# Attention with sinks and a window, then a gated two-layer product: the choice between two code paths is moved from the front of the kernel to its end

## The chip, the cores and the metric

The kernel runs on one core of one Trainium2 chip. The metric is the device time of one execution in microseconds (us). The core has five engines that run programs of their own and meet at semaphores: TensorE (PE; its loads of the stationary operand have a row of their own, PEld), VectorE (DVE), ScalarE (ACT), GpSimd (POOL) and SyncE (SP), which here does nothing but issue DMA transfers. A row whose engine ends in q (SPq, DVEq) shows what that engine's sequencer does by itself: issuing DMAs, loading registers, branching.

## The reference

Four sequences of 768 positions with 8 heads of 64 go through attention. A query sees the first n_sink = 4 keys and the last window = 128 keys up to itself; both numbers are inputs of the kernel. The heads side by side are the rows of x (3072 x 512), which go through a gated product of two matrices (512 x 2048 and 2048 x 512).

```python
scores = scale * np.matmul(q, k.transpose(0, 1, 3, 2))
is_sink = pos[None, :] < int(n_sink)
rel = pos[:, None] - pos[None, :]
in_window = (rel >= 0) & (rel < int(window))
scores = np.where(is_sink | in_window, scores, -1000000000.0)
scores = scores - np.max(scores, axis=-1, keepdims=True)
a = np.exp(scores)
a = a / (np.sum(a, axis=-1, keepdims=True) + 1e-09)
x = np.matmul(a, v)          # heads side by side: 3072 x 512
h = x @ w_in                 # 3072 x 2048
g = h - np.tanh(h)
out = g @ w_out              # 3072 x 512
```

## The kernel before, in words

**Two paths.** `_banded` is written for few sinks and a window of at most 128; `_general` computes the same for any numbers. The kernel loads n_sink and window into registers of all five engines (L82), works out from them whether the banded path may be taken (`bad`, L85), and branches (L94): a compare-and-branch in front of `_banded` that falls through into it, and behind `_banded` an unconditional jump past `_general` to the kernel's end (L1231). Both carry the line number L94. With this case's inputs the banded path runs.

**Units, chunks and steps.** A chunk is 256 queries of one sequence (12 chunks); a unit u is a chunk's two-head pair (4 per chunk, 48 in all). For each unit PE forms the scores (L530 for the first 12 units, which work on f32 keys and queries as they come; L537 later), VectorE merges them with the mask (L558; where a unit has keys from an earlier block, L552 first copies a triangle), ACT takes the exponential (L566), VectorE sums and inverts (L586, L587), the weights are scaled and transposed (L627), VectorE masks the transposed pieces into `pt` (L641), and PE multiplies with the values (L762, L768). ACT and VectorE split the result x into a high part xh and a low part xl (L805: two halves of a chunk, so six L805 for the first three chunks). The two-matrix part is cut in steps n = (chunk, weight group g): 24 products h (L877: xh and xl with the weights `w0_g`), tanh (L882), difference (L885), high and low part of the gate (L889, L893), then 12 products o (L929, with the weights `w1_g`); the first three steps are (chunk 0, g 0), (chunk 1, g 0), (chunk 2, g 0), step 3 is (chunk 2, g 1).

**Weights.** The matrices come packed. For each of 16 pieces (k = 0 or 1 for the matrix, g = 0 to 7) VectorE decodes in three instructions (`_decode_part`, L164, L166, L168), ACT casts the high part, VectorE subtracts it to get the low part (L854). So VectorE has four instructions of 128x1024 for each piece, all on the way to a step's products.

**What sets the order.** All this work is listed by `work.add(engine, duration, due, function, reads, writes, lands=...)`, with durations and due times in ns written by hand. `Work.order` plays it through with these numbers, each engine's time beginning at `BEGIN`, takes at each point the waiting piece with the earliest due time, and hands out one fixed order for each engine; the instructions are then issued in that order. `lands` is what a DMA issue keeps its queue busy in this model.

```python
BEGIN = {"PE": 0.0, "ACT": 500.0, "DVE": 1900.0, "POOL": 400.0, "SP": 1900.0}
...
work.add(engine, 500, t, keys, (), [slots(u)[0], "seq k"], lands=800)
work.add(engine, 1000, t, queries, (), [slots(u)[1], "seq q"], lands=600 if raw(u) else 1000)
...
work.add("DVE", 1000, 3000, rest, (), ["mask"])
```

**The start.** Ahead of `_banded`, in an order written by hand, SP loads the numbers for the masks (L74) and keys and queries of units 0 and 1 (L77 and `_load_pair`, L105: the two heads' 64 rows in two transfers), VectorE builds the parts of the masks that the first merges need, PE runs three products of the identity, and every engine loads the registers and branches. The rest of the masks (`rest`, L145 to L149, five short instructions) is a piece of `work`. On SP the values (L398), the sink values `vraw` (L452, one for each sequence, which overwrites a buffer that VectorE's L467 reads) and the packed weights follow. The 12 early units (`raw(u)`) have a DMA each for keys and two for queries (L370).

**The end.** ACT copies the last chunk's sums out of PSUM, SP stores them (L945), and each engine jumps (L94) to the closing semaphore waits of L1231.

## Time and profile before

| | |
|---|---|
| time, median of 3 runs | 650.28 us (650.25 to 650.84) |
| span of the profiled execution | 650.5 us |
| PE busy | 632.6 us (97%), 4858 products |
| DVE busy | 441.8 us (68%) |
| ACT busy | 354.7 us (55%) |
| POOL busy | 59.8 us (9%) |

The median is that of three runs; every row further down is from one profiled execution, whose span of 650.5 us is 0.2 above the median. The busy shares are averages over the span: the first 60 us, in which attention for the first three chunks and the first weights are made, and the long stretch behind them, in which PE works off steps, differ, so the rows below are cut by stretch. Instructions are pipelined, so the next one on an engine often starts a little before the one ahead of it ends; the distance from start to start is what an instruction keeps its engine.

### The profile page before, as it was taken

To read this page: it belongs to the slowest core of one execution; us is meant where nothing else is said; L and a number is where in the kernel's file an instruction comes from. 1 tells how busy PE (TensorE), PEld (TensorE's weight loads), DVE (VectorE), ACT (ScalarE), POOL (GpSimd) and SP (SyncE) were. 2 spreads that over 40 slices of the span, in tenths; PEclk is the share of its full clock that TensorE was granted. 3 is DMA by queue.
4 is the path that set the end of the run, shared out by engine and by line. 5 is a ranking of instruction groups with operands and counts; after the bars stand their busy time and mean duration, and the time that the engine had idled before them with its cause. 6 is when DMAs were issued, how large, how long until landed. Compare 5 with 4: busy or idle time off the path is not lost.

```text
span 650.5 us, 13450 instructions
## 1 busy us (share of the span) xinstructions
PE 632.6 (97%) x4858; PEld 563.9 (87%) x4858; DVE 441.8 (68%) x1169; ACT 354.7 (55%) x949; POOL 59.8 (9%) x191
## 2 busy tenths in 40 slices
PE   7799999999999999999999999999999999999996
PEld 4467999998989999999989989989999999889995
DVE  6999999957976676856767766666676675642221
ACT  4774444447856556646557557566565565532221
POOL 3663100000000010000010000001000000000000
PEclk9899999999999999999999999999999999999999
DMA  6789920013544344234234233334242342210001
GB/s 199 255 271 333 369 80 0 2 62 108 157 123 151 82 123 146 76 97 143 76 110 151 72 101 117 92 101 120 86 130 86 102 123 66 82 50 1 33 1 37
DMA packets 75350, 73.45 MB, mean 113 GB/s; under 512 B 21132, under 2 KB 62732, under 8 KB 75276
## 3 DMA queue, kind: packets, MB, share of 16 engines
q1 hardware_dynamic: 74972, 72.18, 35.9%
q8 instruction: 40, 0.66, 0.4%
q10 hardware_dynamic: 304, 0.33, 0.2%
q14 instruction: 34, 0.28, 0.1%
HBM read 55.58 MB, written 16.91 MB: 111 GB/s over the span
## 4 chain that ended last, share of the span: by engine, by line
PE 85%; DVE 4%; SPq 3%; ACT 3%; DMA 2%; issue 1%; POOL 1%; ACTq 0%; DVEq 0%; POOLq 0%
PE o L929 38%; PE h L877 36%; PE s L537 5%; PE x L789 4%; DMA turned<-pt 1%; PE x L768 1%; ACT p L566 1%; ACT p L597 1%; DMA qk<-qd 1%; SPq L684 1%; PE s L530 1%; PE x L779 1%; DVE p L558 1%; DMA z<-sinks 1%; PE t L627 1%
## 5 line engine op out<-in xcount | busy, mean ns | idle before, releaser
L877 PE MATMUL h<-xh,w 128*128 128x256 f32 x1536 | 275.6, 277 | 0.0
L877 PEld LDWEIGHTS h<-xh,w 128*128 128x128 f32 x1536 | 237.4, 188 | 2.8 <-issue 1.0
L877 PE MATMUL h<-xl,w 128*128 128x256 f32 x768 | 212.2, 276 | 0.0
L929 PE MATMUL o<-w,gh 128*128 128x512 f32 x768 | 194.0, 393 | 1.1 <-DVE w L854 0.5
L929 PEld LDWEIGHTS o<-w,gh 128*128 128x128 f32 x768 | 137.3, 188 | 27.2 <-issue 1.4
L877 PEld LDWEIGHTS h<-xl,w 128*128 128x128 f32 x768 | 144.3, 188 | 1.7
L885 DVE TENSOR_TENSOR h<-h,graw 128x512 f32<-128x512 f32 x96 | 66.5, 692 | 67.4 <-ACT graw L882 67.3
L566 ACT ACTIVATE p<-p,st 128x132 f32<-128x132 f32 x192 | 76.3, 398 | 53.0 <-DVE st L558 51.4
L929 PE MATMUL o<-w,gl 128*128 128x512 f32 x384 | 103.0, 390 | 0.0
L882 ACT ACTIVATE graw<-h 128x512 f32<-128x512 f32 x96 | 57.2, 596 | 76.4 <-PE h L877 75.9
L893 DVE TENSOR_TENSOR gl<-h,gh 128x512 fp32r<-128x512 f32 x96 | 65.5, 683 | 34.0 <-ACT gh L889 33.9
L889 ACT CAST gh<-h 128x512 fp32r<-128x512 f32 x96 | 55.9, 582 | 57.9 <-DVE h L885 57.9
L929 PEld LDWEIGHTS o<-w,gl 128*128 128x128 f32 x384 | 71.9, 188 | 15.2
L552 DVE COPY_PREDICATED s<-above,s 128x256 f32<-128x256 uint32 x76 | 32.4, 426 | 48.5 <-PE s L537 46.4
L558 DVE CUSTOM_DVE_ANT_0 p<-s,mask 128x132 f32<-128x132 f32 x192 | 48.9, 292 | 8.2 <-PE s L530 2.8
L602 POOL CAST z<-p 128x16 fp32r<-128x16 f32 x48 | 11.3, 236 | 455.1 <-ACT p L597 386.6
L597 ACT ACTIVATE p<-p,st 128x132 f32<-128x132 f32 x144 | 46.6, 394 | 7.6 <-DVE st L587 6.9
L537 PEld LDWEIGHTS s<-ks,q 128*128 128x128 f32 x288 | 42.3, 188 | 5.3 <-issue 0.8
L537 PE MATMUL s<-ks,q 128*128 128x260 f32 x288 | 46.0, 283 | 0.7 <-DVE ks L494 0.5
L494 DVE TENSOR_TENSOR ks<-kraw,ks 64x392 fp32r<-64x392 f32 x72 | 40.5, 562 | 2.3
L499 ACT CAST q<-qraw 128x512 fp32r<-128x512 f32 x36 | 22.4, 623 | 32.6 <-PE s L537 29.2
L489 ACT CAST ks<-kraw 64x392 fp32r<-64x392 f32 x72 | 37.2, 517 | 0.9
(87 smaller groups left out, 503.9 us busy)
## 6 DMA issues: line engine op xcount, KB each, us to landing
qraw<-qd SPq DMA_DIRECT2D x36, 256.0 KB, 2.7
turned<-pt SPq DMA_DIRECT2D x36, 256.0 KB, 2.0
pt<-turned SPq DMA_DIRECT2D x144, 64.0 KB, 2.0
wraw<-w_in SPq DMA_DIRECT2D x16, 512.0 KB, 7.5
wraw<-w_out SPq DMA_DIRECT2D x16, 512.0 KB, 6.1
kraw<-kp SPq DMA_DIRECT2D x37, 196.0 KB, 2.7
out<-ob SPq DMA_DIRECT2D x24, 256.0 KB, 2.5
v<-vp SPq DMA_DIRECT2D x42, 128.0 KB, 2.9
```

Of the source, the lines that this page charges most:

```text
L489: nc.scalar.copy(ks[u][r, h, :], kt[u][r, :])
L494: nc.vector.tensor_tensor(k[o, h, :], t[r, :], k[r, h, :].bitcast(F32), op=ALU.subtract)
L537: nc.tensor.matmul(ps[h][:, :WIN], lhsT=q[:, h, t * P : (t + 1) * P], rhs=rhs, start=i == 0, stop=i == 1,)
L558: nc.vector.tensor_tensor_reduce(out=pr[u][:, j, :], in0=ps[h][:, P:WIN], in1=mask[:, kind, :], scale=-0.125, scalar=BIG, op0=ALU.add, op1 ...
L566: nc.scalar.activation(e, e, AF.Exp, bias=st[u][:, j : j + 1], scale=-1.0, accum_out=st[u][:, 4 + j : 5 + j],)
L597: nc.scalar.activation(pr[u][:, j, :], pr[u][:, j, :], AF.Copy, scale=s[:, 8 + j : 9 + j])
L877: nc.tensor.matmul(y, lhsT=w, rhs=x, start=r == 0, stop=r == 11)
L882: nc.scalar.activation(gr[n], hps[n], AF.Tanh)
L885: nc.vector.tensor_tensor(hps[n], hps[n], gr[n], op=ALU.subtract)
L889: nc.scalar.copy(gh[n], hps[n])
L893: nc.vector.tensor_tensor(gl[n], hps[n], gh[n].bitcast(F32), op=ALU.subtract)
L929: nc.tensor.matmul(y, lhsT=(gh, gh, gl)[i][n][:, f, t * P : (t + 1) * P], rhs=w, start=first and not low and r == 0, stop=bool(last and lo ...
```

## The change

The register loads and the choice of path move behind `_banded`, which now always runs; `_general` runs behind it if the numbers ask for it, and overwrites the output. The queries of the 12 early units come in one transfer of 128 rows. In the planner SP and VectorE begin at 0, and an early unit's query load counts 500 instead of two times 600.

```diff
@@ tile_attention_moe_kernel
-            _load_pair(nc, q, qd[0, 2 * m : 2 * m + 2, :, :CH])
+            _load_pair(nc.sync, q, qd[0, 2 * m : 2 * m + 2, :, :CH])
...
-        _, (nlo, nhi, wlo, whi) = nc.values_load_multi_w_load_instructions(
-            nsw[0:1, 0:4], skip_runtime_bounds_check_because="every value takes one of the two branches"
-        )
-        bad = nhi | whi | ((nlo + 3) >> 3) | ((wlo - 1) >> 7)
...
-    with tc.If(bad == 0) as cmp:
-        _banded(tc, qd, kp, vp, vs, masks, w_in, w_out, ident, pts, early, out)
-    with cmp.Else():
+    _banded(tc, qd, kp, vp, vs, masks, w_in, w_out, ident, pts, early, out)
+    with tc.manual_schedule(engines={et.PE, et.SP, et.DVE, et.Activation, et.Pool}):
+        _, (nlo, nhi, wlo, whi) = nc.values_load_multi_w_load_instructions(
+            nsw[0:1, 0:4], skip_runtime_bounds_check_because="every value takes one of the two branches"
+        )
+        bad = nhi | whi | ((nlo + 3) >> 3) | ((wlo - 1) >> 7)
+    with tc.If(bad != 0):
         _general(tc, qd, kp, vp, nswi, w_in, w_out, ident, xd, out)
@@ _load_pair
-def _load_pair(nc, q, src):
-    for h in range(2):
-        r = slice(64 * h, 64 * h + 64)
-        nc.sync.dma_start(q[r], src[h, r])
+def _load_pair(engine, q, src):
+    engine.dma_start(q, src.rearrange("h r s -> (h r) s")[P // 2 : P // 2 + P])
@@ Work
-    BEGIN = {"PE": 0.0, "ACT": 500.0, "DVE": 1900.0, "POOL": 400.0, "SP": 1900.0}
+    BEGIN = {"PE": 0.0, "ACT": 500.0, "DVE": 0.0, "POOL": 400.0, "SP": 0.0}
@@ load_qk
                 if raw(u):
-                    for h, r in enumerate(HALF):
-                        queue.dma_start(qt[u][r], src[h, r])
+                    _load_pair(queue, qt[u], src)
...
-            work.add(engine, 1000, t, queries, (), [slots(u)[1], "seq q"], lands=600 if raw(u) else 1000)
+            work.add(engine, 500 if raw(u) else 1000, t, queries, (), [slots(u)[1], "seq q"], lands=500 if raw(u) else 1000)
```

The new numbers make the planner hand out another order for the first steps. In the rows that follow, of the programs as they are issued, the changed kernel's line numbers are lower by 2 (mask and decode code: L162, L164, L166 stand for L164, L166, L168) or by 3 (L638 for L641, L765 for L768, L802 for L805, L851 for L854, L874 for L877, L890 for L893, L926 for L929). In names, `w0_1` is the first matrix's group 1, `xl2` is xl of chunk 2, `x2_2` its second half in PSUM, `h2` and `h3` belong to steps 2 and 3, and numbers behind the last underscore only count buffers.

VectorE around the last of the six L805, before:

```order
L166 SCALAR_TENSOR_TENSOR pt_60<-wraw0_1_494,pt_60 128x1024
L893 TENSOR_TENSOR gl1_943<-h1_793,gh1_923 128x512
L168 SCALAR_TENSOR_TENSOR pt_60<-wraw0_1_494,pt_60 128x1024
L164 TENSOR_SCALAR pt_60<-wraw1_1_609 128x1024
L805 TENSOR_TENSOR xl2_884<-x2_2_909,xh2_883 128x512
L166 SCALAR_TENSOR_TENSOR pt_60<-wraw1_1_609,pt_60 128x1024
L854 TENSOR_TENSOR w0_1_957<-pt_60,w0_1_957 128x1024
L168 SCALAR_TENSOR_TENSOR pt_60<-wraw1_1_609,pt_60 128x1024
L164 TENSOR_SCALAR pt_60<-wraw0_2_708 128x1024
```

The same place on VectorE after the change (`w0_1`'s L851 stands some way ahead of the first row here):

```order
L802 TENSOR_TENSOR xl2_794<-x2_0_723,xh2_793 128x512
L890 TENSOR_TENSOR gl1_830<-h1_612,gh1_804 128x512
L164 SCALAR_TENSOR_TENSOR pt_60<-wraw1_1_412,pt_60 128x1024
L638 TENSOR_TENSOR pt_60<-t11_834,below_77 128x2x128
L638 TENSOR_TENSOR pt_60<-t11_834,after_78 128x2x128
L166 SCALAR_TENSOR_TENSOR pt_60<-wraw1_1_412,pt_60 128x1024
L162 TENSOR_SCALAR pt_60<-wraw0_2_511 128x1024
L164 SCALAR_TENSOR_TENSOR pt_60<-wraw0_2_511,pt_60 128x1024
L851 TENSOR_TENSOR w1_1_874<-pt_60,w1_1_874 128x1024
L802 TENSOR_TENSOR xl2_794<-x2_2_839,xh2_793 128x512
```

Both matrices' group 1 and the first two decode instructions of group 2 now stand ahead of the second half of `xl2`; before, only a part of group 1 did.

PE at the second half of chunk 2's values product, before:

```order
L762 MATMUL x2_2_909<-zr_260,vsink_257 128x512
L768 MATMUL x2_2_909<-pt_60,v2_0_800 64x256 x2
L768 MATMUL x2_2_909<-pt_60,v2_1_802 64x128 x2
L768 MATMUL x2_2_909<-pt_60,v2_0_800 64x256 x2
L768 MATMUL x2_2_909<-pt_60,v2_1_802 64x128 x2
L929 MATMUL o1_948<-w1_0_860,gh1_923 128x512
L929 MATMUL o1_948<-w1_0_860,gh1_923 128x2x8x32
L929 MATMUL o1_948<-w1_0_860,gh1_923 128x512 x6
L929 MATMUL o1_948<-w1_0_860,gl1_943 128x512 x4
L877 MATMUL h2_925<-xh2_883,w0_0_537 128x256
L877 MATMUL h2_925<-xl2_884,w0_0_537 128x256
L877 MATMUL h2_925<-xh2_883,w0_0_537 128x256 x2
```

The same place on PE after the change:

```order
L759 MATMUL x2_2_839<-zr_174,vsink_171 128x512
L765 MATMUL x2_2_839<-pt_60,v2_0_672 64x256 x2
L765 MATMUL x2_2_839<-pt_60,v2_1_674 64x128 x2
L765 MATMUL x2_2_839<-pt_60,v2_0_672 64x256 x2
L765 MATMUL x2_2_839<-pt_60,v2_1_674 64x128 x2
L926 MATMUL o1_825<-w1_0_532,gl1_830 128x512 x2
L874 MATMUL h3_881<-xh2_793,w0_1_753 128x2x4x32
L874 MATMUL h3_881<-xl2_794,w0_1_753 128x256
L874 MATMUL h3_881<-xh2_793,w0_1_753 128x256 x2
L874 MATMUL h3_881<-xl2_794,w0_1_753 128x256
L874 MATMUL h3_881<-xh2_793,w0_1_753 128x256
L874 MATMUL h2_842<-xh2_793,w0_0_359 128x256
```

Ten of the twelve `o1` products now stand ahead of `x2_2`, and six of step 3's products, which use the first half of `xl2`, stand between it and the remaining products of step 2, which use the second half.

SP at the end, before:

```order
L945 DMA out<-ob11_0_7872 128x512
L945 DMA out<-ob11_1_7877 128x512
L94 UNCONDITIONAL_BRANCH
L1051 DMA graw0_0_7907<-w_in 128x2048
L1051 DMA graw1_0_7913<-w_out 128x2048
```

And after (what follows here, as above, is the general path):

```order
L942 DMA out<-ob11_0_7776 128x512
L942 DMA out<-ob11_1_7781 128x512
L92 TENSOR_LOAD nsw_ptr
L92 TENSOR_LOAD nsw
L96 REGISTER_ALU
L96 ISA
L96 REGISTER_ALU
L96 ISA
L96 REGISTER_ALU
L96 COMPARE_AND_BRANCH
```

The two register loads and the branch that stood ahead of the first values on SP now stand behind the last store, and the compare-and-branch is the one that leads past the general path.

## Rows read from the trace of the kernel before

**Rows 1.** First line of the page.

```profile
span 650.5 us, 13450 instructions
```

**Rows 2.** Busy time by stretch: us and instructions of each engine, clock, DMA share, GB/s.

```profile
0.00:8.60 8.60, 4.80 (x18) 3.57 (x18) 4.78 (x31) 2.17 (x5) 2.06 (x12) 1.00 0.47 122
8.60:62.32 53.72, 47.37 (x323) 32.66 (x320) 48.57 (x182) 37.74 (x135) 29.09 (x59) 0.97 0.87 288
62.32:160.00 97.68, 97.68 (x650) 89.40 (x649) 84.41 (x122) 45.57 (x84) 2.29 (x6) 1.00 0.31 105
160.00:644.67 484.67, 482.76 (x3875) 438.22 (x3873) 304.02 (x838) 268.66 (x726) 26.36 (x114) 1.00 0.32 95
```

**Rows 3.** Timeline of PE: start, duration, line, operation, out<-in, count.

```profile
4.97 2.44 PE L530 MATMUL s<-pt 64*128 64x260 f32 x8
...
63.65 0.28 PE L877 MATMUL h<-xh,w 128*128 128x256 f32 x1
...
68.60 0.63 PE L929 MATMUL o<-w,gh 128*128 128x512 f32 x2
```

**Rows 4.** Chain of waits in order of time, its start: start, duration, what.

```profile
2.29 0.59 SPq L105
...
4.71 1.19 SPq L82
...
7.04 0.34 SPq L398
```

**Rows 5.** Timeline of VectorE at its first merge, idle time before it in brackets.

```profile
7.23 0.30 DVE L558 CUSTOM_DVE_ANT_0 p<-s,mask 128x132 f32<-128x132 f32 x1 [2.32 <-PE s L530]
...
7.67 0.22 DVE L145 COPY mask<-mask 128x128 f32<-128x128 f32 x1
```

**Rows 6.** VectorE's waits from 0 to 62.32: us in total, times, longest.

```profile
DVE p L558 <- PE s L530: 2.8, 2, 2.3
DVE s L552 <- PE s L530: 1.7, 3, 1.1
...
DVE pt L641 <- ACT pt L634: 1.0, 2, 0.5
```

**Rows 7.** Timeline of VectorE around the sixth L805.

```profile
61.03 0.69 DVE L164 TENSOR_SCALAR pt<-wraw 128x1024 uint32<-128x1024 uint32 x1
61.63 0.68 DVE L805 TENSOR_TENSOR xl<-x,xh 128x512 fp32r<-128x512 f32 x1
62.23 1.22 DVE L166 SCALAR_TENSOR_TENSOR pt<-wraw,pt 128x1024 uint32<-128x1024 uint32 x1
63.36 1.22 DVE L854 TENSOR_TENSOR w<-pt,w 128x1024 fp32r<-128x1024 f32 x1
64.50 1.22 DVE L168 SCALAR_TENSOR_TENSOR pt<-wraw,pt 128x1024 uint32<-128x1024 uint32 x1
```

**Rows 8.** Timeline of SP at the end.

```profile
643.95 1.69 SPq L945 DMA_DIRECT2D out<-ob  x2
```

**Rows 9.** Single lines: duration in ns (least/median/most), first and last start.

```profile
L945 SPq DMA_DIRECT2D out<-ob x24: 332/356/377, 142.8 to 645.3; - x24
...
DMA to landing us min/median/max: 2.0/2.5/4.3
...
L82 ACTq TENSOR_LOAD <-nsw x1: 1578/1578/1578, 1.6 to 1.6; - x1
...
L82 SPq TENSOR_LOAD <-nsw x1: 507/507/507, 5.9 to 5.9; - x1
...
L94 SPq COMPARE_BRANCH  x2: 38/46/53, 6.9 to 645.7; - x2
L94 DVEq COMPARE_BRANCH  x2: 50/56/63, 7.0 to 641.3; - x2
...
L1231 SPq EVENT_SEMAPHORE  x8: 17/28/28, 648.6 to 650.4; - x8
...
L1231 DVEq DRAIN  x2: 10/25/40, 644.2 to 650.0; - x2
```

## The prediction

> **What bounds the kernel now.** I read the page's first line first: the profiled execution spans 650.5 us [rows 1], 0.2 above the median of 650.28; all sums below are made against 650.5 and brought down by 0.2 at the end. Then busy time by stretch [rows 2]: the reader is to see that PE is busy for all 97.68 us from 62.32 to 160, and idle for only 1.91 of the 484.67 us after that. From 62 us on PE is the bound and simply works off its list. Whatever the change is worth in front is therefore read at one question: at what time does PE stand where it stood at about 64 us? Before that, VectorE is the fuller engine: it has idled 3.82 us by 8.60, and from there to 62.32 it is busy 48.57 of 53.72 us, 90%, while its last piece of attention for this stage still lies ahead of PE's [rows 2].
>
> The last thing PE needs from attention in this stage is the second half of xl of chunk 2 (the sixth L805). In the kernel before PE did not wait for it: it went on at 63.65 behind other work, with 18 products of step 2 and 24 of step 3 to do until 68.60, 0.118 us each [rows 3].
>
> **The change part by part.**
>
> The register loads and the branch in front go. On SP's part of the chain the loads start at 4.71 and the next transfer starts at 7.04: 2.33 us in which SP issues nothing [rows 4]. On VectorE a wait of 2.32 us stands before the first merge at 7.23, and the profile puts it down to PE [rows 5]. But VectorE's own branch is at 7.0 [rows 9], while PE began the first four products at 4.97 and took 2.44 us [rows 3], so the first two were there at about 6.2. The gap is VectorE's loads, and the merge can start about 0.95 us earlier. Besides, the rest of the masks (five short instructions from 7.67 to 8.60, where the first stretch of [rows 2] ends, 0.93 us [rows 5]) now stands ahead of that merge, where VectorE has nothing to do anyhow. Together VectorE gains 1.9 us at the start. The loads on PE, ACT and POOL cost nothing before: PE waits there for unit 0's data, ACT for scores, POOL has no work; their removal gives nothing.
>
> A pair's early queries in one transfer instead of two: one issue of about 0.6 us less per unit on SP (the second half's issue at 2.29 took 0.59 [rows 4]). For units 0 and 1 it brings data some tenths earlier, but PE's products at low speed follow each other without a gap there; I count nothing beyond the 0.95 above. Later units' transfers are issued well ahead, so these savings lie under VectorE's work.
>
> The planner. Because a query load is now half as long for it, and SP and VectorE begin at 0 in its model, it hands out another order up to step 6. That is the largest term, and it is read from the order of VectorE. Ahead of the sixth L805 stand the same instructions as before and six more, all of them weight work: one L164, two L166, one L168, two L854. From the kernel before: an L164 keeps VectorE for 0.60 us (61.03 to 61.63), an L166 for 1.13 (62.23 to 63.36), an L854 for 1.14 (63.36 to 64.50), and an L168 is taken like the L854 [rows 7]. That is 0.60 + 2 x 1.13 + 3 x 1.14 = 6.3 us. The sixth L805 ended at 61.63 + 0.68 = 62.3; with these ahead it ends at 68.6, less what VectorE idles less.
>
> What it idles less has two parts. The 1.9 us of the start are as good as certain. Of the later waits for another engine, the longest of the three kinds are 1.1, 0.5 (2.8 less the 2.3 of the start) and 0.5 us [rows 6], 2.1 in all; the order around them is another one, the weight work that comes earlier can stand where VectorE waited, but new waits of that kind can come. The first units stay a chain from product to merge to exponential and keep their short ones. I count half, 1.05. The bounds: none of it, so 1.9; all waits of the three kinds, 0.5 + 1.7 + 1.0 = 3.2 more, so 5.1. With 2.95 the sixth L805 ends at 65.65, and PE goes on 0.1 later, at 65.75.
>
> In the new order PE has by then done six products of step 3 that came later before, so the same amount of work was left to it at 63.65 + 6 x 0.118 = 64.36. PE's whole remaining list is therefore 1.4 us later (bounds 2.4 later and 0.7 earlier). Before the step moved, PE's cover for xl was the second half of step 1; that cover now runs out some 2 us before xl is there. Behind it PE's order is the old one, and VectorE, with its weights done earlier, is no longer close behind PE, so I let the shift stand until the end. The 1.91 us of PE idle after 160 I leave as they are.
>
> The end. Every engine now loads the registers and branches after its last instruction. For PE, ACT, VectorE and POOL this starts earlier than SP's and is covered by it. SP ends its last store's issue at 643.95 + 1.69 = 645.64 [rows 8]. Before, its jump is at 645.7 and its next instruction at 648.6, 2.9 us on; the last store, issued at 645.3, lands up to 4.3 us later, at 649.6, and ends the kernel 0.9 us after that [rows 9]. So the jump lay under the landing. Now SP runs the loads first, 2.33 us as at the start [rows 4], and then jumps: 645.64 + 2.33 + 2.9 = 650.9. That is 1.3 us after the landing, and the short semaphore waits that were passed under it, 0.2 to 0.3 us, come on top: 1.6 us. VectorE jumps alike, from 641.3 to 644.2 with nothing to wait for [rows 9], so the 2.9 us are the jump and not a wait. Bounds: above, one load took 1.58 us on ACT and 0.51 on SP [rows 9], 1.1 more, so 2.7; below, the branch in front that is not taken (6.9 on SP, next transfer at 7.04 [rows 4, 9]) costs 0.1, SP would be through at 648.1 under the landing, and the end would cost nothing. I take 1.6, since the jump at the end leads past the same general path as the one measured there.
>
> [...]
>
> One wait changes its place. On SP the third load of vraw, which waits for VectorE's L467, stands ahead of unit 8's keys and queries now (before: behind unit 9's). Behind it in SP's queue are units 8 and 9 and the weights of group 2. VectorE has between that L467 and unit 8's first merge an L805, an L168, an L854 and the merges and masks of unit 7, which cover most of a transfer's issue and landing. I count nothing and keep it for the upper side; uncovered, I put it at 1 to 2 us, a choice.
>
> Sum: 650.5 + 1.4 + 1.6 = 653.5 for a profiled execution, less 0.2: **653.3 us**, slower by 0.46%.
>
> **The rivals.** (0.2%, 1.3 us, is about what a measurement of this kernel can tell from no change.)
>
> *The start's chain carries through* (faster). SP's part of the chain gets shorter by 2.33 us of loads and by four issues of second halves of 0.6 us (units 0, 1, 3 and 4) [rows 4], 4.7 us. If the transfers, and not VectorE, set the pace until 62 us, all of that reaches PE, and with the end's 1.6 us the time is 647.2. For it speaks that the chain runs over SP up to unit 5's load; against it that VectorE is busy 90% of the time from 8.60 on and has 6.3 us more to do first. It decides where the sixth L805 ends before about 61.4.
>
> *The end is hidden, or VectorE makes up nearly everything.* If the jump is short, 651.7; if VectorE saves 4.5 to 5.1 us, 651.1 to 651.7; both together would be no change. The 1.91 us of PE's late waits may also shrink and lead here.
>
> *VectorE saves nothing beyond the start, or waits anew* for unit 8's loads: PE is 2.4 us later or, with 1 to 2 us for the loads, 3.4 to 4.4; the time is 654.3 to 656.3.
>
> *The new order does nothing* to PE's pace, because weight work fills waits that were there anyway: only the end counts, 651.9. It needs 4.3 us of waits saved, more than the start gives.
>
> **How the numbers follow.** Forecast as worked out (652 to 655): 0.56. End hidden, VectorE making up nearly everything, or the order without effect (650.3 to 652): 0.23, of which 0.15 within 0.2%. More waits (above 654.3, half of it above 655.4): 0.13. Chain carried through: 0.08. So faster 0.08, within 0.2% 0.16, slower 0.76. The range 650.6 to 655.4 leaves out the faster case, a few hundredths of the second and half of the third, under 0.2.
>
> **What would show it.** The first merge at about 6.3 us with the masks' rest ahead of it; the sixth L805 ending between 65 and 67 us, with a PE wait of 1 to 2 us before the next L877; step 2's first L929 at about 70 instead of 68.6; PE without waits from there to 160; the last L929 ending about 1.4 us later; on SP some 2.3 us of loads after the last store's issue, then 2.9 us to its next record, which now comes after the landing. The prediction is wrong if the sixth L805 ends before 64 us or after 68, or if SP's record after the branch is there before the last store lands.

## The result, and the profile after

The changed kernel takes 659.31 us (median; 658.87 to 659.79) against 650.28: slower by 9.0 us, ratio 1.0133 (95% interval 1.0119 to 1.0148; the two medians by themselves give 1.0139). The forecast was 653.3, and the range ended at 655.4.

The profiled span grows from 650.5 [rows 1] to 656.9, so the two traces hold 6.4 us of the 9.0. The rest lies in the baseline: in the runs beside the experiments each execution of the kernel before took 1.77 to 1.96 us more than its own span, 1.85 on average (a span of 650.5 went with 652.35 us), so the profiled execution, whose own time is not on record, was by this one of the longer ones, 2.1 above the median; the changed kernel's takes 2.2 more than its span (659.14 at 656.9), 0.4 more than before's. 6.4 + 2.1 + 0.4 + 0.2 (659.31 over 659.14) are the 9.0, but for roundings.

First line of the changed kernel's page, to set beside [rows 1]:

```profile
span 656.9 us, 13426 instructions
```

Busy time by the stretches of [rows 2], same columns:

```profile
0.00:8.60 8.60, 3.96 (x16) 2.94 (x18) 5.06 (x31) 1.85 (x4) 1.86 (x12) 1.00 0.64 206
8.60:62.32 53.72, 42.10 (x288) 29.80 (x287) 48.55 (x179) 36.84 (x133) 29.34 (x57) 0.94 0.80 277
62.32:160.00 97.68, 96.85 (x644) 87.43 (x643) 79.76 (x106) 42.16 (x70) 5.33 (x6) 1.00 0.28 97
160.00:644.67 484.67, 483.45 (x3895) 439.84 (x3894) 307.29 (x853) 272.64 (x740) 27.40 (x117) 1.00 0.32 96
```

The loss is made before 62 us: PE does 42.10 us of work there instead of 47.37, VectorE is as busy as before (48.55 against 48.57). Behind 62 us PE works off its list as before.

Timeline of PE: the first scores, the wait for xl, and step 2's first L926 (L929 in [rows 3]); the idle time before an instruction stands in brackets:

```profile
6.29 2.10 PE L527 MATMUL s<-pt 64*128 64x260 f32 x8 [2.38 <-DMA pt<-qd]
...
69.73 0.39 PE L874 MATMUL h<-xl,w 128*128 128x256 f32 x1 [0.67 <-DVE xl L802]
...
74.14 1.20 PE L926 MATMUL o<-w,gh 128*128 128x512 f32 x4 [0.16 <-ACT gh L886]
```

Timeline of VectorE at the first merge [rows 5] and at the sixth xl [rows 7]:

```profile
5.55 0.22 DVE L143 COPY mask<-mask 128x128 f32<-128x128 f32 x1
...
7.69 0.29 DVE L555 CUSTOM_DVE_ANT_0 p<-s,mask 128x132 f32<-128x132 f32 x1 [0.93 <-PE s L527]
...
67.86 1.22 DVE L851 TENSOR_TENSOR w<-pt,w 128x1024 fp32r<-128x1024 f32 x1
68.99 0.68 DVE L802 TENSOR_TENSOR xl<-x,xh 128x512 fp32r<-128x512 f32 x1
```

The masks' rest (L143) did move ahead, but the first scores begin at 6.29 instead of 4.97, held by the landing of unit 0's queries, and the first merge at 7.69 instead of 7.23. The sixth xl ends at 68.99 + 0.68 = 69.67 instead of 62.31; PE waits 0.67 us for it, reaches step 2's L926 5.5 us later than before (74.14 against 68.60), and its last product ends 4.8 us later (649.45 against 644.66).

VectorE's busy time from 0 to the end of the sixth xl, the kernel before first, the changed kernel second (columns as in [rows 2]):

```profile
0.00:62.31 62.31, 52.16 (x337) 36.23 (x338) 53.34 (x211) 39.90 (x140) 31.16 (x71) 0.97 0.81 265
```

```profile
0.00:69.67 69.67, 52.81 (x349) 37.97 (x349) 59.90 (x217) 41.94 (x143) 34.55 (x73) 0.95 0.73 248
```

So up to this point VectorE worked 59.90 - 53.34 = 6.56 us more in six more instructions, and idled 69.67 - 59.90 = 9.77 us where it had idled 62.31 - 53.34 = 8.97.

The end, by single lines (duration in ns, first and last start), to set beside [rows 9]:

```profile
L942 SPq DMA_DIRECT2D out<-ob x24: 332/357/1304, 148.4 to 650.1; - x24
...
L92 SPq TENSOR_LOAD <-nsw_ptr x1: 1067/1067/1067, 650.5 to 650.5; - x1
L92 SPq TENSOR_LOAD <-nsw x1: 602/602/602, 651.6 to 651.6; - x1
...
L96 SPq EVENT_SEMAPHORE  x8: 17/17/17, 655.2 to 655.7; - x8
...
L96 SPq COMPARE_BRANCH  x1: 54/54/54, 652.6 to 652.6; - x1
...
L1228 SPq EVENT_SEMAPHORE  x8: 17/28/28, 655.8 to 656.9; - x8
```

The store is issued at 650.1, two loads take 1.67 us, the branch is at 652.6 and SP's next record at 655.2, eight semaphore steps follow, and the kernel ends at 656.9: 7.5 us behind PE's last product, where it was 5.8.

### The profile page after: what moved, and what is told of

Read it like the earlier page. It is cut to its first block, busy times and chain, and to the rows that moved or that the text cites. A ratio compares the mean times of both kernels' runs of the same rounds, so it can differ in the third digit from the quotient of the medians.

```text
span 656.9 us, 13426 instructions
## 1 busy us (share of the span) xinstructions
PE 631.1 (96%) x4858; PEld 563.6 (86%) x4858; DVE 442.0 (67%) x1169; ACT 355.3 (54%) x949; POOL 63.9 (10%) x191
## 4 chain that ended last, share of the span: by engine, by line
PE 85%; DVE 6%; ACT 4%; issue 1%; SPq 1%; DMA 1%; POOL 1%; ACTq 0%; DVEq 0%
PE o L926 38%; PE h L874 36%; PE s L534 5%; PE x L786 4%; ACT p L563 1%; PE s L527 1%; DVE p L555 1%; ACT p L594 1%; DVE pt L164 1%; DMA pt<-qd 1%; PE x L776 1%; DVE pt L166 1%; DVE s L549 1%; DVE pt L638 1%; PE x L765 0%
## 5 line engine op out<-in xcount | busy, mean ns | idle before, releaser
L874 PE MATMUL h<-xh,w 128*128 128x256 f32 x1536 | 277.1, 278 | 0.0
L874 PEld LDWEIGHTS h<-xh,w 128*128 128x128 f32 x1536 | 238.5, 189 | 2.1 <-issue 0.3
L874 PE MATMUL h<-xl,w 128*128 128x256 f32 x768 | 212.7, 277 | 0.7 <-DVE xl L802 0.7
L926 PE MATMUL o<-w,gh 128*128 128x512 f32 x768 | 193.4, 393 | 0.3 <-ACT gh L886 0.2
L926 PEld LDWEIGHTS o<-w,gh 128*128 128x128 f32 x768 | 137.4, 188 | 25.9 <-issue 1.0
L874 PEld LDWEIGHTS h<-xl,w 128*128 128x128 f32 x768 | 144.8, 189 | 2.5 <-DVE xl L802 0.9
L926 PE MATMUL o<-w,gl 128*128 128x512 f32 x384 | 103.2, 390 | 0.0
L890 DVE TENSOR_TENSOR gl<-h,gh 128x512 fp32r<-128x512 f32 x96 | 65.6, 683 | 34.7 <-ACT gh L886 34.6
L926 PEld LDWEIGHTS o<-w,gl 128*128 128x128 f32 x384 | 71.9, 188 | 15.3 <-issue 0.2
```

Source lines behind the costliest of these rows:

```text
L874: nc.tensor.matmul(y, lhsT=w, rhs=x, start=r == 0, stop=r == 11)
L890: nc.vector.tensor_tensor(gl[n], hps[n], gh[n].bitcast(F32), op=ALU.subtract)
L926: nc.tensor.matmul(y, lhsT=(gh, gh, gl)[i][n][:, f, t * P : (t + 1) * P], rhs=w, start=first and not low and r == 0, stop=bool(last and lo ...
```

## The experiments

The first theories: A, the new order puts weight work ahead of the sixth xl, and so PE is late; B, the loss comes from the start, where transfers collide; C, the time outside the span grows with the branch at the end. Later came F (weight work ahead of the fifth xl), H (SP's order) and L (the lead of the scores over the rest of the attention). "Order" below is what the planner hands out. Each time stands beside runs of the kernel before on the same chip; ratios are to those.

**The branch alone at the end.** The kernel before with these two pieces behind `_banded`:

```diff
-        _, (nlo, nhi, wlo, whi) = nc.values_load_multi_w_load_instructions(...)
-    with tc.If(bad == 0) as cmp:
+    _banded(...)
+    _, (nlo, nhi, wlo, whi) = nc.values_load_multi_w_load_instructions(...)
+    with tc.If(bad != 0):
```

> The kernel before, with nothing but the register loads and the branch moved behind the banded path; query loads, planner numbers and so every engine's order are those of before. Theory A (the new order of VectorE's weight work made the loss, PE 4.8 us later at its last instruction): PE ends within 1 us of before (644.7), the span grows by the tail alone, 1.65 us, to 651 to 652.5. Theory B (without the loads in front the first transfers run into each other, and the start is what was lost): PE ends at about 649, the span is about 656. For the 2.2 us by which the changed kernel's time exceeds its span: theory C (they come with the branch at the end) has time minus span at about 2.2 here; theory D (they come from the order or the transfers) has it at -0.2.

653.47 us, ratio 1.0040 (1.0025 to 1.0054); PE's last product ends at 644.1, the tail is 7.7, time minus span 2.1. The move by itself costs 2.7 us, and PE, without the loads in front, is hardly earlier (644.1 against 644.66).

**The branch alone back in front.** The changed kernel with loads and branch in the old place.

> The changed kernel with the register loads and the branch put back in front; the new planner numbers, its order and the merged query transfers stay. Theory A: PE's last instruction ends 4 to 7 us later than before, the span is 655 to 657 with before's tail. Theory B: the start is before's, PE ends within 1 us of before, span 650 to 651.5. Theory C: time minus span -0.2. Theory D: 2.2.

658.44 us, 1.0104 (1.0077 to 1.0131); PE's last product ends at 651.9, the sixth xl at 72.5. Most of the loss stays, and the sixth xl is no earlier than in the changed kernel: the loss is made by the new order and not, as theory B had it, at the start.

**The old numbers.** The changed kernel with BEGIN and query loads as the planner had them before, so with the old order.

> The changed kernel with the planner numbers of before (1900 at the start, 1000 and 600 for a query load), so with before's order on every engine; branch at the end and merged query transfers stay. Theory A: like the kernel with only the branch moved, span 651 to 652.5. Theory B: span about 656, and, if the merged transfers are what collides, longer than with two transfers. Theory C: time minus span 2.2. Theory D: -0.2 if the order is at work, 2.2 if the transfers are.

653.69 us, 1.0043 (1.0026 to 1.0059), like the branch alone. One transfer for a pair's queries is worth nothing that can be measured here, and the new order costs some 5.6 us, 659.3 less 653.7.

**No branch.** Loads, branch and general path left out; the kernel computes the banded path alone.

> The changed kernel without register loads, branch and general path (it computes the banded path alone). Both theories on PE: PE ends as in the changed kernel, at about 649.5; the tail is before's or shorter, so the span is 655 to 655.3, 1.65 to 2 less than the changed kernel's 656.9. Theory C: time minus span goes back to -0.2, so the time is about 655. Theory D: it stays at 2.2, the time is about 657.4.

654.27 us, 1.0052 (1.0036 to 1.0067). PE is as late as expected (last product 650.6), but the tail is 3.7 us, shorter than before's 5.8: without the jump past the general path the kernel ends about 2 us sooner behind PE than the kernel before, which has it (1.4 to 2.7, since the tail is 5.0 to 6.3 us in the three traces with the branch in front). Time minus span went to 1.8, so theory C; but it is a small term, 2.1 to 2.2 with the branch at the end and 1.85 in the kernel before.

**The register loads earlier**, with the old order, the branch still at the end:

```diff
+LATE = 40
...
+            for i, n in enumerate(todo):
+                if i == len(todo) - LATE:
+                    bad = _choice(nc, nsw)
                 work.all[n][3]()
```

> The kernel with the order and transfers of before and the branch behind the banded path, its register loads moved ahead of the last 40 pieces of the planner's list, so on SP ahead of the last two stores, where SP waits for ACT anyway; branch and jump stay at the end. If the tail is the chain of SP's loads (1.67 us), their arithmetic (0.4) and the jump (2.6), the tail gets 2.1 us shorter than with the loads behind the store (7.7), so 5.6, and the time is 651.1 to 651.7. If the store's landing or the jump alone ended it, the tail stays above 7 and the time at 653 to 653.7. Should PE, VectorE or ACT be held up by their own loads, PE's end moves up to 2 us later and the time is 652 to 653.5 with a tail of 5.6.

652.06 us, 1.0027 (1.0013 to 1.0042); the tail is 5.8, where 5.6 was forecast for loads and jump in a row, and the time is a little above the forecast.

**ScalarE holds back unit 2's loads**, on top of the last one:

```diff
+                if u == 2:
+                    nc.scalar.copy(gap[:, 0:1], qt[0][:, 0:1])
                 queue.dma_start(kt[u], ...)
```

> The kernel with the old order, branch at the end and early register loads (652.06), with one thing more: ScalarE copies one column of unit 0's queries before it issues unit 2's loads, so these start after unit 0's data have landed, as they started later in the kernel before (3.85 us). If these loads in the way of unit 0's were what ate the gain at the start, unit 0's first product starts at 4.9 to 5.3 instead of 6.0, the first merge at 6.4 to 6.9 instead of 7.7, the sixth xl ends about 1 us earlier than 62.0 and the time is 650.8 to 651.4. If SP's own next transfers (values, weights) are what is in the way, the first product stays at 5.9 or later and the time at 652.

651.44 us, 1.0008 (0.9991 to 1.0025). Timeline of PE:

```profile
4.54 2.96 PE L537 MATMUL s<-pt 64*128 64x260 f32 x8 [0.63 <-DMA pt<-qd]
```

Unit 0's data come 1.5 us earlier (4.54 against 6.0) and the first merge starts at 6.8 instead of 7.7: unit 2's loads, which ScalarE issues from 0.75 us on when it has no registers to load, were in the way. But the sixth xl ends at 62.6 (62.0 without). A first merge that is 0.9 us earlier did not reach it. This is the best version with the branch at the end, and no faster than the kernel before.

**The second weight groups behind the sixth xl**, for the planner alone, in the changed kernel (the planner makes its whole list anew, and the calls that list the attention of chunks 1 and 2 move ahead of these weights):

```diff
+                first = [("xu", 2, 2)] if (k, g) in ((1, 1), (0, 2)) else []
-                ... bits(i), [("wr", k, g, 0), ("wr", k, g, 1)], ...
+                ... bits(i), [("wr", k, g, 0), ("wr", k, g, 1)] + first, ...
```

> The changed kernel with one dependence added for the planner alone: the decoding of weight groups (second matrix, 1) and (first matrix, 2) may only start behind the second half of xl of chunk 2. Ahead of the sixth xl subtraction VectorE then has 12.0 us of weight instructions instead of 17.7 (11.4 in the kernel before), the order up to group 1's first piece stays the changed kernel's. Theory A (the weight work ahead of this xl is what delays PE, about 1 us per us): the sixth xl ends near 64, PE ends 5 to 6 us earlier, time 653 to 654.5. Theory E (the rest of the new order, its waits at the first units, lost the time): less than 1.5 us is won, time 657.8 to 659.5.

660.31 us, 1.0139 (1.0103 to 1.0174). VectorE up to the end of the sixth xl:

```profile
0.00:69.37 69.37, 54.72 (x346) 39.01 (x347) 54.09 (x211) 40.52 (x142) 31.61 (x72) 0.93 0.73 247
```

Theory A, on which the forecast stood, falls: 5.8 us of work were taken away (54.09 against 59.90), and the xl is there at 69.37 instead of 69.67. The work's place was filled with idle time (15.3 us).

**Only a part of the new numbers.** The zero start with the old query loads:

> The changed kernel with the old planner numbers for a query load (1000 and 600) and the new zero start of SP and VectorE. Its order has 14.8 us of weight instructions ahead of the sixth xl subtraction, 2.9 less than the changed kernel's and 3.4 more than before's. Theory A: time between the changed kernel's 659.3 and the 653.6 of the kernel with the old order, at 656 to 657.5. Theory E: no order in it; as likely near 659 as near 653.6.

658.62 us, 1.0129 (1.0101 to 1.0158): above theory A's interval. VectorE's zero start alone:

> The changed kernel with only VectorE's start in the planner at 0; SP's start and the query loads have the numbers of before. 10.8 us of weight instructions stand ahead of the sixth xl subtraction, 0.6 less than before. Theory A: 652.5 to 654, like the kernel with the old order or half a us better. Theory E: any other time, since the order of the first units is another one again.

654.63 us, 1.0071 (1.0048 to 1.0095). Less weight work ahead goes with less time among these plans, but not throughout: this one has 0.6 us less of it than the old order (1.0043) and is no faster, and the run before these two has 5.7 us less than the changed kernel and takes as long. No cause is shown by this.

**The kernel before again.**

> The kernel before, unchanged, for a second profile of it. The forecast was made against a profiled execution with a span of 650.5 us; the other executions of the same kernel had spans of 648.0 to 651.0 and times 1.85 us above their spans. If the first profile was one of the long ones, this one has a span near 648.7, its granted clock is nearer to 1, and PE ends about 1 us earlier than 644.7, the tail is under 5.8. If it was typical, all of these are as in the first profile.

651.03 us beside 651.08, ratio 1.0002. The second profile has again a span of 650.5, at a clock of 0.991; its time is 652.35 and the eight executions have spans of 648.2 to 651.6. The first profile was thus a usual one of the longer half, and it is the time outside the span that the forecast had overlooked.

**The first weight group behind the fifth xl as well.**

> As the kernel whose second weight groups wait for the sixth xl (660.3 us), and the decoding of group (first matrix, 1) waits for the fifth xl as well: 8.0 us of weight instructions ahead of the fifth xl instead of 12.0 (before: 8.6), the same 12.0 ahead of the sixth. Theory F (weight instructions that stand between the merges and sums of the units ahead of the fifth xl lengthen attention's chain; those between the fifth and the sixth lie in a wait): the fifth xl ends 3 to 4 us earlier than the 62.8 there, the sixth 2.5 to 4 earlier than 69.4, the time is 656 to 657.8. Rival E (the first units' order and the start): less than 1 us is won.

661.93 us, 1.0161 (1.0139 to 1.0183). The fifth xl came 3.4 us earlier (59.4), as theory F said, the sixth 1.7 later (71.1): in this run's plan six products of step 3 stand ahead of chunk 2's second values product (in the changed kernel they stand behind it), and PE waited 0.75 us in them for these weights. Theory F's time is missed.

**PE filled in its two long waits**, in the changed kernel:

```diff
+                for _ in range(8 if u in (5, 9) else 0):
+                    nc.tensor.transpose(ps[:, 0, 0, :], ident, ident)
```

> The changed kernel with eight transposes of the identity put ahead of the transposes of units 5 and 9, where PE waits 2.4 and 2.6 us for GpSimd; their results are overwritten by those that follow. Theory G (PE's low clock after these two waits, 0.5 from 34.0 to 37.4 and from 51.1 to 54.5, slows the products on the chain to the sixth xl): the low stretches go, the sixth xl ends 1.5 to 3 us earlier, time 656.5 to 658. Theory F (the waits are a result of VectorE's order and the low clock costs little): time within 1 us of 659.3.

657.70 us, 1.0101 (1.0082 to 1.0120), some 2 us less than the changed kernel (1.0133 on both chips it ran on). In the changed kernel the granted clock is 0.50 in these two stretches, at PE's waits of 2.41 us (to 32.93) and 2.60 us (to 51.72) for GpSimd (columns as in [rows 2], the clock is the third number from the end):

```profile
34.01:37.40 3.39, 3.14 (x14) 2.75 (x16) 2.65 (x6) 1.51 (x4) 2.57 (x4) 0.50 0.58 137
51.07:54.47 3.40, 2.75 (x13) 2.75 (x14) 3.18 (x11) 1.73 (x9) 1.25 (x4) 0.50 0.99 336
```

The first wait was not filled: the fill products themselves had to wait, 2.41 us for VectorE until 33.18, and the low stretch is there as it was (32.75 to 36.14). At the second place the wait is 1.38 us ahead of them, and the low stretch is gone. The sixth xl ends at 69.0, where two profiles of the changed kernel have 69.67 and 70.47.

What the clock is worth can also be read from executions with different clocks. Of the ten without a branch the two with a mean clock of 0.999 and more took 652.5 and 652.7 us, the eight at 0.992 653.9 to 656.2. But the second profile of the kernel before has 10.2 us at 0.50 ahead of its sixth xl, which ends at 62.94 even so; and one profile of a kernel further down (weights as before, SP's new order) has none, and its xl ends at 68.06. In that order:

```profile
0.00:62.94 62.94, 52.27 (x337) 36.27 (x338) 53.49 (x211) 39.86 (x140) 31.06 (x71) 0.92 0.82 269
```

```profile
0.00:68.06 68.06, 51.54 (x343) 34.91 (x343) 52.95 (x211) 40.89 (x142) 32.09 (x72) 1.00 0.75 252
```

The clock is a part of the loss, not the main part.

**SP's part of the order against the other engines'.** A list made of two plans, SP's rows from the plan with the old numbers, or all but SP's:

```diff
+    rows = {e: [n for n in (old if e in OLD else new) if work.all[n][0] == e] for e in w.BEGIN}
```

> The changed kernel, its order on PE, VectorE, ScalarE and GpSimd, but on SP the order of transfers that the numbers of before give: the third sink-value load behind units 8 and 9 instead of ahead of them, weights spread between the units' loads. Theory H (SP's order made the loss: units 8 to 11 were issued at 34.1, 36.0, 38.4 and 47.7 us in the changed kernel, at 28.2, 28.9, 33.1 and 34.5 by the old order, and the last halves of attention wait for them): the sixth xl ends 3 us or more earlier than 69.7, time 655 to 656.5. Theory F (the compute engines' order, VectorE's weight work ahead of the fifth xl): less than 1 us is won, 658.3 to 659.5. Both chains equally long: 657 to 658.3, since each holds when the other is mended.

> The other way round: the order of before on PE, VectorE, ScalarE and GpSimd, the changed kernel's order of transfers on SP alone; branch at the end, merged query loads. Theory H: most of the loss is here, 657 to 659.5. Theory F: like the kernel with the old order everywhere (653.7), 653.3 to 654.5. Both chains: 655 to 658.

> The changed kernel once more, on the chip of these two, as the corner with which they are compared, and for a second profile: 658.5 to 659.8, sixth xl at 69 to 70.5, unit 11's keys issued at 47 to 49 us.

On one chip: 658.71 (1.0112, 1.0079 to 1.0146) with SP's old order, 667.14 (1.0256, 1.0225 to 1.0287) with SP's new order alone, 660.14 (1.0133, 1.0108 to 1.0159) with both. So the compute engines' order costs about 5 us by itself (653.7 to 658.7), SP's in the changed kernel some 1.4 more, which the intervals do not tell from nothing. With the old compute order SP's new one costs 13. PE there:

```profile
39.62 2.10 PE L552 MATMUL s<-qk 64*128 64x260 f32 x8 [4.71 <-DMA qk<-qd]
...
57.54 2.02 PE L552 MATMUL s<-qk 64*128 64x260 f32 x8 [4.41 <-DMA qk<-qd]
```

PE waits 4.71 and 4.41 us for the keys and queries of units 8 and 11. The changed kernel's SP, whose order this is, issues unit 8's at 34.07, behind the third sink-value load, and unit 11's at 47.66; the kernel before issues them at 23.66 and 36.72. Changed kernel first, then before:

```profile
33.46 0.56 SPq L449 DMA_DIRECT2D vraw<-vs  x1
34.07 0.46 SPq L356 DMA_DIRECT2D qk<-kp  x1
...
47.66 0.42 SPq L356 DMA_DIRECT2D qk<-kp  x1
```

```profile
23.66 0.43 SPq L358 DMA_DIRECT2D qk<-kp  x1
...
36.72 0.43 SPq L358 DMA_DIRECT2D qk<-kp  x1
```

**Weights as before, attention in a new order** (the one that the planner makes with these ties and the new numbers; it is neither the old one nor quite the changed kernel's), with the order on SP that the old numbers give and with the one that the new ones give:

```diff
+BEHIND = {(0, 0): (0, 0, 1, 1), (1, 0): (2, 3, 4, 4), (0, 1): (4, 5, 5, 6), (1, 1): (5, 6, 6, 6), (0, 2): (6, 6, 6, 6)}
```

> The changed kernel with SP's order of the numbers of before, and VectorE's weight instructions bound, for the planner, to the same places between the six xl subtractions as in the kernel before: 2, 4, 5, 6, 9 and 12 of them ahead of the first to the sixth xl (changed kernel: 3, 6, 8, 10, 13, 18). What stays new is the order of the attention pieces themselves, as the planner makes it with a zero start. Theory F (the weight instructions among the units' merges and sums make the five us that the compute engines' order costs): the sixth xl ends at 62 to 64.5, time 653.5 to 655.5. Rival K (the order of the attention pieces is what costs): the sixth xl stays at 67 or later, time 657 or more.

> The same with the changed kernel's own order on SP. Theory H2 (behind VectorE's work the late loads of units 8 to 11 are a second chain of nearly the same length, hidden in the changed kernel and open once VectorE is quick): time at least 3 us above the run with SP's old order, 657 to 663, with PE waiting 2 to 5 us for a unit's queries. If SP's order does no harm by itself: within 1 us of that run.

662.33 us, 1.0166 (1.0133 to 1.0198), and 662.39, 1.0177 (1.0149 to 1.0205): neither is nearer to the kernel before than the changed kernel is. VectorE up to the end of the sixth xl with the old numbers on SP:

```profile
0.00:71.28 71.28, 57.87 (x343) 38.34 (x343) 53.32 (x211) 40.80 (x142) 32.55 (x72) 0.95 0.70 240
```

It does the work of before (53.32 us in 211 instructions, before 53.34 in 211) and idles 71.28 - 53.32 = 17.96 us. Its waits in that time (us in total, times, longest):

```profile
DVE xl L829 <- ACT xh L825: 3.7, 1, 3.7
DVE pt L665 <- PE t L651: 2.0, 1, 2.0
DVE pt L665 <- ACT pt L658: 1.6, 3, 0.7
DVE p L582 <- POOL z L626: 1.6, 1, 1.6
```

The sixth xl itself now waits 3.7 us for ScalarE. So the weight work that stands ahead is not the sole cause (theory F falls), and with the weights in their old place SP's order makes no difference in time.

**The lead of the scores**, with SP's old order:

```diff
+        for u in range(RAW - 2):
+            work.all[made["t", u]][4].update(made["s", u + 2, t] for t in range(2))
```

> The kernel with the new compute order and SP's old order (658.7), with one thing more bound for the planner: PE may transpose a unit's weights only behind the scores of the unit two further on, as it did in the kernel before nearly throughout (s4 before t2, s8 before t6, s11 before t9; in the new order s4 behind t2, s8 behind t6, s11 behind t9). The planner then puts 19.4 us of weight instructions ahead of the sixth xl subtraction, more than the changed kernel's 17.7. Theory L (what the new order took is the lead of the scores: unit 11's scores began at 55.9 us instead of 46): unit 11's scores begin 3 us or more earlier than 56.9, the sixth xl ends 3 us or more earlier than 70.7, time 653.5 to 656. Theory F (weight instructions ahead of the xl subtractions): the sixth xl at 70 or later, time 658.5 or more.

The last scores of the stage (unit 11's) on PE, in the kernel before, the changed kernel and this one:

```profile
45.80 1.15 PE L530 MATMUL s<-qk 64*128 64x260 f32 x8
```

```profile
55.91 1.15 PE L527 MATMUL s<-qk 64*128 64x260 f32 x8
```

```profile
55.33 0.71 PE L552 MATMUL s<-qk 64*128 64x260 f32 x4 [0.23 <-DVE st L580]
```

In the changed kernel PE makes them 10.1 us later than before. Tied two units ahead, as here, they are hardly earlier (this is their second half), and PE waits for VectorE in front of them. 662.46 us, 1.0182 (1.0152 to 1.0212). VectorE up to the sixth xl, first without the tie (the run with SP's old order), then with it:

```profile
0.00:70.66 70.66, 53.84 (x349) 38.41 (x349) 59.77 (x217) 41.81 (x143) 34.49 (x73) 0.95 0.72 244
```

```profile
0.00:71.64 71.64, 56.27 (x347) 38.82 (x348) 61.72 (x218) 41.63 (x144) 31.25 (x73) 0.95 0.71 239
```

Its idle time fell from 70.66 - 59.77 = 10.89 to 71.64 - 61.72 = 9.92 us, but more work came ahead of the xl, 61.72 - 53.34 = 8.38 us over before. Theory L's forecast is missed; since the last scores did not really come earlier, this does not clear them either.

## Why the prediction was wrong

Its frame held. In every run PE's last product ends 579 to 583 us behind the sixth xl, a spread of 4 us over all orders (before 644.66 - 62.31 = 582.35, changed 649.45 - 69.67 = 579.78), so what counts is when that xl is there. What failed is the step that put it there at 65.65.

**The step that failed.** The forecast added 6.3 us of weight work and took off 2.95 us of saved idle time. The work was sized right: 6.56 us. Of the idle time nothing was saved; it rose by 0.80. The xl came 7.36 us later instead of 3.3, and PE's list was 5.5 us late at step 2's L926 and 4.8 at the last product instead of 1.4. That is 3.4 of the 6.0 us by which the forecast missed.

Nor was VectorE's list ahead of the xl, from which this sum was made, the path that set its time. In every trace the sixth xl starts 0.7 to 1.7 us behind the end of PE's second values product of chunk 2 (L768, now L765), with only ScalarE's xh between them. Before and after the change:

```profile
59.34 1.52 PE L768 MATMUL x<-pt,v 128*64 128x256 f32 x16
60.90 0.59 ACT L801 CAST xh<-x 128x512 fp32r<-128x512 f32 x1 [1.94 <-PE x L768]
```

```profile
66.08 1.52 PE L765 MATMUL x<-pt,v 128*64 128x256 f32 x16
67.65 0.59 ACT L798 CAST xh<-x 128x512 fp32r<-128x512 f32 x1 [0.55 <-PE x L765]
```

The product ends at 67.60 instead of 60.86: 6.74 of the 7.36 us, and VectorE's list adds 0.62. So PE is late before the xl is. Up to the sixth xl PE works 0.65 us more (52.81 against 52.16 in the lines of the section on the result) and idles 16.86 us instead of 10.15. GpSimd scales a unit's weights before PE transposes them, and PE's waits for it there, of which the kernel before lists none, are 7.4 us:

```profile
PE t L624 <- POOL p L589: 5.0, 3, 2.6
PE t L624 <- POOL z L599: 2.4, 1, 2.4
```

The second values product of chunk 0 still ends earlier than before (28.16, before 30.02), the next one later (40.16, 38.07), with the wait of 2.41 us between them; from the second of chunk 1 (47.46, 45.87) to the first of chunk 2 (58.94, 53.46), around the wait of 2.60 us, 3.9 us more are lost. GpSimd itself waits 25.6 us for VectorE's inverses, where it waited 14.9. That weight work delays PE by this way round is read from the trace and not shown by a run: with the scores tied two units ahead PE's waits for GpSimd are down to 0.2 us, others have come, and the xl is as late.

- The 1.9 us of the start, "as good as certain", did not come. The masks' rest did move, but without ScalarE's loads its queue issues unit 2's transfers at 0.75 us, into unit 0's landing. Holding them back showed that (first product at 4.54 instead of 6.0); it also showed that an earlier first merge did not bring the sixth xl earlier, and that VectorE's loads were only a part of the gap: with none in front, and PE's first product 0.43 us earlier than before, the first merge came at 6.78, 0.45 us earlier than before and not 0.95.
- "Half of the later waits" had the wrong sign. In VectorE's waits up to the sixth xl of the changed kernel (columns as in [rows 6]) those for PE are shorter (2.6 us instead of 4.5, with the start's 2.3 gone), those for ScalarE longer (2.6 instead of 1.6), and waits on a DMA and on POOL are new. A line of the kernel before that [rows 6] do not show stands first:

```profile
DVE st L586 <- ACT p L566: 0.6, 2, 0.3
```

```profile
DVE p L555 <- PE s L527: 2.4, 4, 0.9
DVE pt L638 <- ACT pt L631: 1.7, 3, 1.0
...
DVE st L583 <- ACT p L563: 0.9, 2, 0.7
DVE few L134 <- DMA nswi<-nsw: 0.9, 1, 0.9
DVE vsink L464 <- POOL vraw L460: 0.5, 1, 0.5
DVE s L549 <- PE s L527: 0.2, 1, 0.2
```

- Deeper, work and idle time are not two terms. Taking 5.8 us of the work away gave 5.5 us more idle time (54.09 busy, 15.28 idle), taking all of it away 8.2 more than in the changed kernel (53.32 and 17.96), and with the scores tied 1.0 us less idle time came with 1.95 us more work. In all three the sixth xl starts 0.7 to 0.8 us behind PE's values product (68.68, 70.59 and 70.96, behind 68.01, 69.92 and 70.18): what VectorE has no longer to do ahead of the xl, it waits. Of the orders tried, only the old one (the sixth xl at 62.0 to 62.9 in its runs) and the one with VectorE's zero start alone (63.6) have it near its old time.

**What stands, what is open.** The new order of the compute engines costs some 5 us by itself, SP's in the changed kernel perhaps 1.4 more. The branch behind the banded path costs 2.7 us with the order as before. The merged transfer is worth nothing measurable by itself. Which move within the compute engines' order is decisive is open: the weights alone were put back and gave nothing, the attempt on the scores did not make them early, both together were put back only as the whole old order, and no run took away PE's waits for GpSimd by themselves. The low clock at PE's two waits is a part of it; one run with fill products puts half of it at some 2 us, with intervals that touch.

**The end.** The forecast was 1.6 us; the tail grew by 7.49 - 5.81 = 1.68. That this is so near is in part luck. The tail of one and the same program differs from trace to trace (5.8 and 6.3 us in the two of the kernel before), and the parts missed both ways: 2.17 us from the first load to the branch, of which 1.67 are the loads, and 2.56 us from the branch at 652.64 to the next record at 655.20, where 2.33 and 2.9 were forecast, then 1.7 us of closing steps to the end, where the sum left 1.2. The rival of a short jump fell by these 2.56 us. The run without a branch adds what the forecast had not asked: without the jump past the general path the tail is about 2 us shorter than in the kernel before (3.67 against 5.81, or against 5.0 to 6.3 over three traces). That these 2 us are the jump's own time is not shown: in the kernel before SP's next record [rows 9] is there ahead of the last store's landing, which comes 4.2 us after the issue; in the changed kernel this landing takes 2.3 us.

**The baseline.** The forecast set its time 0.2 us below the profiled span. The changed kernel's median lies 2.4 above its own (659.31 at 656.9), since every time that stands on record beside its span is 1.75 to 2.24 us above it, and the profiled execution of before was a long one. That is 2.6 us, and with 3.4 on PE and 0.1 on the tail the 6.0 missed, but for roundings.

**SP's moved wait**, costed at nothing: right for the changed kernel within what the runs can tell (1.4), wrong as a price. With the old order of the other engines, SP's new one costs 667.14 - 653.7 = 13.4 us. In the new order PE comes to unit 8's scores at 40.09 us, where it came there at 34.16 before, which leaves room for the later loads.

**The rivals.** That of new waits came nearest: its upper end has PE 4.4 us late where 4.8 were measured, and with the 2.6 of the baseline its 656.3 become 658.9. But the wait that it named, for unit 8's loads, is not among those of the changed kernel's trace, on PE or on VectorE. The carried-through start and the order without effect fell, both by the xl at 69.67. The chance of slower was 0.76; the range ended 3.9 us too low.

## What to carry to other kernels

When numbers of a planner change, the change is the new order of all engines: work put ahead of a landmark cannot be added up on one engine with the idle time guessed, so look up in a trace which engine's result the landmark waits for, and swap one engine's order at a time before believing a sum. The branch behind the last store was exposed with its loads and its jump, 2.7 us of time and a tail of 7.7 us with the order as before; loads that stood ahead of the last two stores took some 1 us of it back, with a tail of 5.8. Compare a profile's own time with its span, and several executions of the kernel, before one span serves as the baseline.

## What the runs showed of the hardware

- Without register loads, branch and general path the tail was 3.67 us, in the kernel before 5.81 (5.0 to 6.3 in the three traces with the branch in front). From SP's branch past the general path to its next record it took 2.56 us in the changed kernel, 2.6 in the kernel with early loads and 2.9 in the kernel before [rows 9].
- First loads on one queue delayed those on another: with unit 2's issued on ScalarE's (at 0.75 us in the changed kernel) the first product, which needs SP's, starts at 6.29 there and at 6.0 in the kernel with early register loads; with them held back in the latter, at 4.54.
- The first eight score products went slower than later ones of the same form: 2.44 us [rows 3] against 1.15 at 45.80 in the kernel before, both at a granted clock of 1.00.
- Low stretches of PE's clock differ between executions of one program. In the changed kernel two stretches of 3.4 us at a granted clock of 0.50, from 34.01 and from 51.07, stand at waits of 2.41 us (to 32.93) and 2.60 us (to 51.72); the first profile of the kernel before has one of 3.4 us (26.2 to 29.6) behind waits of 1.02 us (to 24.06) and 0.30 us (to 25.36), the second has 6.8 and 3.4 us of it at the same span of 650.5.
- The time outside the span is 1.85 us on average in the kernel before (1.77 to 1.96) and 2.1 to 2.2 with the branch at the end (2.06 to 2.24 in single runs). No run explains it.
